# Filler products into an accumulators' bank and further into the program, and bulk loads entered by the modelled length of the DMA queue

## The chip, the cores and the metric

One core of a Trainium2 chip. The time is device microseconds of one execution of the whole program, median over several executions. The core's engines are TensorE (PE; its weight loads are listed as PEld), VectorE (DVE), ScalarE (ACT), GpSimd (POOL) and SyncE (SP, which here issues every DMA). Each engine runs its own list of instructions in order, and waits on semaphores where it needs another's result.

## The reference

Three stages over 4 batches of 768 tokens, 384 channels:

```python
# 1. linear attention with decay, 8 heads of 48: state (48 x 48) per head
cur = einsum('bhd,bhe->bhde', u[None] * kt, vt)
y[:, :, t] = einsum('bhd,bhde->bhe', rt, state + cur)
state = w[None, :, :, None] * state + einsum('bhd,bhe->bhde', kt, vt)
...
# 2. gated block, mixing over tokens
h = gelu(x @ w_in);  u, v = h[..., :512], h[..., 512:]
v_n = (v - mean) / sqrt(var + 1e-06) * g_ln
v_s = einsum('ts,bsd->btd', w_sg, v_n) + b_sg[None, :, None]
x = x + (u * v_s) @ w_out
...
# 3. causal convolution of 5 taps as a gate
gate = sigmoid(conv5(x));  out = (gate * (x @ w_val)) @ w_out
```

Weights of the second and third stage come as 64-bit floating point words and are turned into a sum of two narrower parts on the chip; every product with them is three matmuls (high by high, high by low, low by high).

## The kernel before

**Attention** goes by chunks of 128 tokens, 24 of them (6 a batch). Chunk i has, on PE: T (`att_T`, L551: transposes of r and of the scaled k, `ks`), S (`S_products`, L575: scores), KV (`KV_products`, L608), dT (L643), the product with the state (L651) and Y (L666: scores by v). DVE turns the transposed r and, for chunk 0, k into `rT` and `kT` (L559; later `kT` is ACT's, L557) and masks the scores (`sc`, L583). POOL makes `ks` (L497) and the diagonal term (`dv`, L526, L527, L535). ACT copies Y to `yT` (L683); SP writes it to a DRAM tile `xd` (L687, L688) and reads it back turned as `xf` (L693), from which ACT and DVE make the two parts of x (`R`, L721 and L725).

**The gated block** of a batch goes by V (6 row blocks, L824 to L826, `pm<-win,R` with 512 columns), U (`pm<-R,win`), SG (`pm<-wsg,vh`), O1 (`pm<-R,wout`), VAL (`pm<-R,w_val`) and O2 (`pm<-w_out,R`). Below, V(4) is V of row block 4 of batch 0, and so on.

**Weights.** `prepare` loads a block of 64-bit words (`Rst`, L351) and turns it: ACT reads the words first (`warm<-Rst`, L339, into a scratch in PSUM, `pw`), DVE does L340 to L342, then the two parts are written (L365, L373). `w_sg` is loaded as `st` (L393); ACT sums its squares (L397), `ssb` is the sum's copy (L409), and a small PE product with ones (`scale_w_sg`, L418) gives the scale by which `w_sg` is cast (`psg`, L447, L455) and transposed by DMA (L450). `load_conv` (L266) loads the convolution's taps as words, `cwd`, in three DMAs of 5 KB; ACT's first step on them is `cwt<-cwd` (L339).

**The order** of every engine's list is made when the program is built, by a planner with a clock of its own in modelled ns. PE takes the next ready task of two streams (attention and block); every other piece of work is a step of a *chain*, with the engines that may do it, a cost, a priority and what it needs. `next_step` picks the step that can start first, then by priority, `advance` writes it into its engine's list. `"Q"` is SP's list; `self.dma` is the time at which the modelled DMA queue runs empty. Where no PE task is ready, `go` moves the clock to the next event and writes filler products (bf16 ones by ones, 128 columns, result never read) for a share of the gap. Filler products keep PE from standing still, and nothing else. The tile that they write is `warm`: before, the columns from `TH` = 384 on of the bank `pw`, the same bank whose first 384 columns are the words' scratch. PSUM has 8 banks here: `pw`, four `pa` for attention, three `pm` for the block's accumulators.

Of the kernel before, what the change touches and what calls it, by code (L numbers as in the profile page):

```python
# [6 lines left out]
F32 = mybir.dt.float32  # L7
# [10 lines left out]
P = 128  # L18
# [8 lines left out]
TH = 384  # L27
# [4 lines left out]
class Kern:  # L32
# [28 lines left out]
    def mark(self, key, t=None):  # L61
        self.end[key] = self.pe_end + LAT if t is None else t

    def give(self, tok, n=1, t=None):
        self.tok[tok] += [self.pe_end + LAT if t is None else t] * n

    def chain(self, key, *steps, after=(), prio=1):

        self.left[key] = self.left.get(key, 0) + 1
        self.n_chain += 1  # L70
        self.chains.append([self.pe_end + LAT, prio, self.n_chain, key, list(steps), list(after)])

# [18 lines left out]
    def next_step(self):  # L91
        best = None
        for c in self.chains:
            engs, ns, f, *res = c[4][0]
            t = self.when(res[0] if res else (), c[5], c[0])
            if t is None:
                continue
            for e in engs:
                cost = step_ns(e, ns)
                s = max(t, self.free[e])  # L100
                if holds(e, engs, ns):
                    s = max(s, self.port)
                if e == "A" and isinstance(ns, tuple) and ns[0] != self.table:
                    s, cost = s + HOLD[ns[0]], cost + TURN
                k = (s, c[1], s + cost, c[2])
                if best is None or k < best[0]:
                    best = (k, c, e, cost)
        return best

    def advance(self, t):  # L110

        while True:
# [10 lines left out]
            if holds(e, engs, ns):  # L123
                self.port = s + cost
            c[0] = s + cost + LAT
            if e == "Q":
# [20 lines left out]
    def go(self, streams, choose):  # L147

        live = [[] for _ in streams]
        self.done = [0.0] * len(streams)  # L150
        while True:
            for n, (gens, window) in enumerate(streams):
                while len(live[n]) < window and gens:
                    g = gens.pop(0)
                    live[n].append([g, next(g)])
            if not any(live):
                return
            times = [[self.when(t[1][2], t[1][1], self.now) for t in ts] for ts in live]
            ready = [next((i for i, t in enumerate(ts) if t is not None and t <= self.now), None) for ts in times]
            n = choose(ready)  # L160
            if n is None:
                best = self.next_step()
                soon = [t for ts in times for t in ts if t is not None]
                if best is not None:
                    soon.append(max(best[0][0], self.now))
                assert soon, ("stuck", [t[1] for ts in live for t in ts], [(c[3], c[5], c[4][0][3:]) for c in self.chains])
                t = min(soon)
                for _ in range(int((t - self.now) * (FILL0 if self.now < 14000 else FILL) / (112 if self.now < 4000 else 56)) if self.now < FILL_END else 0):

                    nc = self.nc  # L170
                    nc.tensor.matmul(self.pw[:, TH:], self.onesb, self.onesb, start=True, stop=True)
                self.now = self.pe_end = t
                self.advance(self.now)
                continue
            i = ready[n]
            g, (ns, after, taken) = live[n][i]
            self.take(taken)
            self.pe_end = self.now + ns
            req = next(g, None)
            if req is None:  # L180
                live[n].pop(i)
            else:
                live[n][i][1] = req
            self.done[n] += ns
            self.now = self.pe_end
            self.advance(self.now)
# [26 lines left out]
    def consts(self):  # L213
        nc = self.nc
        self.ident = self.const([P, P], F32, "ident")
        make_identity(nc, self.ident)
        self.mask = self.const([P, P], BF16, "mask")
        nc.gpsimd.memset(self.mask, 1.0)
        nc.gpsimd.affine_select(
            out=self.mask, in_=self.mask, pattern=[[1, P]], base=-1, channel_multiplier=-1,  # L220
            compare_op=ALU.is_ge, fill=0.0,
        )
        self.exps = self.const([P, 1], F32, "exps")
        self.onesb = self.const([P, P], BF16, "onesb")
        nc.vector.memset(self.onesb, 1.0)

        nc.scalar.copy(self.exps, self.onesb[:, 0:1])
        nc.vector.memset(self.exps, -0.5)
        self.rp = [self.const([P, H, 64], F32, f"rp{i}") for i in range(NL)]
        self.kp = [self.const([P, H, D], F32, f"kp{i}") for i in range(NL)]  # L230
        self.ks = [self.const([P, H, 64], F32, f"ks{i}") for i in range(2)]
        for t in self.rp + self.ks:
            nc.vector.memset(t[:, :, D:], 0.0)
        self.junk = self.const([P, H, D], BF16, "junk")
        self.dvp = [self.const([P, H, 64], F32, f"dv{i}") for i in range(2)]
        for t in self.dvp:
            nc.gpsimd.memset(t[:, :, D:], 0.0)
        self.T = [self.const([HR, NP, HR], F32, f"T{i}") for i in range(2)]
        for t in self.T:
            nc.gpsimd.memset(t, 0.0)  # L240
        if WARM:

            self.pw = self.pa.tile([P, 512], F32, tag='pw', name='warm', bufs=1)
            for _ in range(WARM):
                nc.tensor.matmul(self.pw[:, TH:], self.onesb, self.onesb, start=True, stop=True)

    def load_w(self):
        nc = self.nc
# [864 lines left out]
    def run(self):  # L1113
        nc = self.nc
# [16 lines left out]
        for i in range(B * NCH):  # L1131
            self.att_new(i)
        self.chain("small", ("Q", (2, 1300), lambda e: self.load_small()), prio=2, after=[("ld", AFTER_SM)])
        self.chain("conv", ("Q", (12, 1100), lambda e: self.load_conv()), prio=2, after=[("ld", AFTER_CW), "small"])
        self.prepare_sg(PR_SG)
        for i in range(NCH):
            self.parts_sg(i, PR_PS)
# [25 lines left out]
def step_ns(e, n):  # L1163

    if isinstance(n, float):
        return n
    if e == "Q":
        return 1175.0 if n[0] == "T" else 475.0 * n[0]
    if isinstance(n, dict):
        return n[e]  # L1170
    if isinstance(n, tuple):
        return n[1]
    return {"V": 69 + 1.042 * n, "A": 93 + 0.833 * n, "P": 165 + 2.06 * n}[e]
# [14 lines left out]
AFTER_SG, AFTER_SM, AFTER_CW = 6, 6, 9  # L1188
WA, WM = 3, 4
NW = 3  # L1190
NR, NS, NA, NX, NY, NL, NV, NPA = 12, 10, 3, 3, 2, 3, 2, 4
WARM = 1
LAT = 130.0
A_FIRST, M_FIRST, RATE = 29000.0, 15000.0, 0.43
TOKENS = {"R": NR, "W": NW, "S": NS, "A": NA, "xf": NX, "yT": NY, "sc": 2, "pw": 1, "pa": NPA, "pm": 7 - NPA}
# [4 lines left out]
HOLD_G, HOLD_S, TURN = 200.0, 0.0, 1280.0  # L1200
HOLD = {"gelu": HOLD_G, "sigmoid": HOLD_S}
FILL, FILL0 = 0.4, 0.8
FILL_END = 9000.0
TAIL = [(1, 0, 0), (1, 0, 1), (1, 0, 2), (0, 1, 0), (0, 1, 1), (0, 1, 2), (2, 0, 0), (2, 0, 1), (1, 1, 0), (1, 1, 1), (1, 1, 2), (2, 0, 2), (2, 1, 0), (2, 1, 1), (2, 1, 2)]
W_LEAST, W_MOST = 0.75, 1.0
N_OK = HR * NP
# [42 lines left out]
```

## Time and profile before

| | |
|---|---|
| three executions | 470.57 us median (470.04 to 470.74) |
| profiled execution | 471.12 us, its span 469.4 us, mean granted clock 0.981 |
| PE | 445.6 us busy, 95% of the span, 3365 matmuls |
| DVE | 348.6 us, 74% |
| ACT | 204.7 us, 44% |
| POOL | 200.2 us, 43% |
| DMA | 41.35 MB |

The span runs from the first to the last instruction; the profiled execution's own time is 1.7 us longer. The granted clock is the share of TensorE's full clock (2.4 GHz) that the chip grants it; 0.50 is the lower of its two levels, 1.2 GHz. A busy share over the whole span is an average over a start in which PE is short of work and a long rest in which it is not.

### The profile page before, as it was taken

How to read it: one execution, taken by the hardware profiler on the slowest of the kernel's cores; microseconds unless marked ns; L12 is line 12 of the kernel's file. 1: busy time of each engine (PE TensorE's matmuls, PEld its weight loads, DVE VectorE, ACT ScalarE, POOL GpSimd, SP SyncE). 2: the span in 40 equal slices, each digit the busy share in tenths (PEclk: the TensorE clock that was granted, in tenths of full speed). 3: DMA queues.
4: the chain of work that ended last, by engine and by line, in shares of the span. 5: the costliest groups of instructions: out<-in, count | busy, mean ns of one | idle time of the engine just before them, and what ended most of it. 6: DMA issues, size and time to landing. Idle time of an engine off the chain costs nothing.

```text
span 469.4 us, 8848 instructions
## 1 busy us (share of the span) xinstructions
PE 445.6 (95%) x3365; PEld 378.6 (81%) x3365; DVE 348.6 (74%) x687; ACT 204.7 (44%) x441; POOL 200.2 (43%) x236
## 2 busy tenths in 40 slices
PE   6988987999998999999999998999999999999996
PEld 6776876968876999887877997987777989777895
DVE  7598958899998685677687766765488684559982
ACT  3547498725452465443143434741123374203142
POOL 4778375635469016664753364644011121300000
PEclk9799898999999899999999999999999999999999
DMA  7999975886243325332223333300000301000002
GB/s 149 234 228 229 268 214 112 172 201 168 53 85 67 103 52 135 85 73 49 52 50 86 103 68 92 94 1 0 3 1 19 116 0 52 0 2 0 1 34 73
DMA packets 116272, 41.35 MB, mean 88 GB/s; under 512 B 89344, under 2 KB 114048, under 8 KB 116224
## 3 DMA queue, kind: packets, MB, share of 16 engines
q1 hardware_dynamic: 116224, 40.73, 35.9%
q8 instruction: 28, 0.46, 0.4%
q14 instruction: 20, 0.16, 0.1%
HBM read 28.92 MB, written 9.44 MB: 82 GB/s over the span
## 4 chain that ended last, share of the span: by engine, by line
PE 72%; DVE 12%; DMA 4%; POOL 3%; ACT 3%; issue 3%; SPq 1%; DVEq 0%; POOLq 0%; ACTq 0%
PE pm L824 20%; PE pm L825 19%; PE pm L826 19%; PE pa L575 4%; PE pa L666 3%; PE pa L551 3%; PE pa L651 2%; DVE R L725 2%; DVE sc L583 1%; DVE warm L945 1%; DMA cwd<-in_moe_conv_w_dram 1%; DMA Rst<-in_moe_w_in_dram 1%; PE pa L608 1%; DVE S L340 1%; DVE S L341 1%
## 5 line engine op out<-in xcount | busy, mean ns | idle before, releaser
L824 PE MATMUL pm<-wsg,vh 128*128 128x384 f16 x192 | 62.8, 327 | 0.5 <-DVE S L911 0.5
L826 PE MATMUL pm<-wsg,vh 128*128 128x384 f16 x192 | 62.6, 326 | 0.0
L825 PE MATMUL pm<-wsg,vh 128*128 128x384 f16 x192 | 62.6, 326 | 0.0
L945 DVE SCALAR_TENSOR_TENSOR warm<-xf,cw,warm 128x384 f32<-128x384 f32 x72 | 44.6, 619 | 7.2 <-ACT warm L943 5.9
L623 ACT ACTIVATE T<-T,W 112x112 f32<-112x112 f32 x80 | 27.0, 383 | 32.2 <-DVE T L617 32.0
L497 POOL TENSOR_TENSOR ks<-kp,tabS 128x384 f32<-128x384 f32 x24 | 24.5, 1020 | 37.2 <-PE pa L608 31.7
L911 DVE SCALAR_TENSOR_TENSOR S<-pm,gs,b_bc 128x384 f32<-128x384 f32 x32 | 19.7, 616 | 22.9 <-PE pm L826 22.7
L825 PE MATMUL pm<-R,wout 128*128 128x384 f32 x96 | 32.9, 343 | 1.5 <-DVE R L889 1.4
L824 PE MATMUL pm<-R,win 128*128 128x384 f32 x96 | 34.4, 358 | 0.0
L824 PE MATMUL pm<-R,wout 128*128 128x384 f32 x96 | 34.2, 357 | 0.0
L850 POOL TENSOR_TENSOR rs<-rs,exps 128x1 f32<-128x1 f32 x24 | 13.3, 556 | 48.6 <-DVE rs L847 48.5
L881 ACT ACTIVATE S<-pm 128x384 f32<-128x384 f32 x32 | 15.7, 490 | 41.9 <-PE pm L826 37.4
L826 PE MATMUL pm<-R,wout 128*128 128x384 f32 x96 | 32.5, 339 | 0.0
L575 PE MATMUL pa<-rT,kT 48*128 48x128 f32 x384 | 29.0, 291 | 3.6 <-ACT kT L557 1.7
L826 PE MATMUL pm<-R,win 128*128 128x384 f32 x96 | 32.3, 336 | 0.0
L825 PE MATMUL pm<-R,win 128*128 128x384 f32 x96 | 32.3, 336 | 0.0
L889 POOL TENSOR_TENSOR R<-xf,R 128x384 fp32r<-128x384 f32 x10 | 10.1, 1013 | 50.6 <-ACT R L1177 30.1
L863 DVE BATCH_NORM_STATS2 bst<-A 128x6 f32<-128x512 f32 x24 | 16.6, 692 | 18.9 <-ACT A L862 18.7
L824 PE MATMUL pm<-win,R 128*128 128x512 f32 x72 | 30.3, 421 | 0.0
L824 PEld LDWEIGHTS <-vh 128*128 128x128 f16 x192 | 18.7, 98 | 13.5 <-issue 2.7
L575 PEld LDWEIGHTS pa<-rT,kT 48*128 48x128 f32 x384 | 24.4, 193 | 6.5 <-ACT kT L557 3.0
L826 PEld LDWEIGHTS <-vh 128*128 128x128 f16 x192 | 18.8, 98 | 12.7 <-DVE vh L868 0.4
(181 smaller groups left out, 1272.1 us busy)
## 6 DMA issues: line engine op xcount, KB each, us to landing
rp<-in_r_dram SPq DMA_DIRECT2D x24, 192.0 KB, 3.4
kp<-in_k_dram SPq DMA_DIRECT2D x24, 192.0 KB, 3.9
v<-in_v_dram SPq DMA_DIRECT2D x24, 192.0 KB, 3.0
xd<-yT SPq DMA_DIRECT2D x48, 96.0 KB, 2.2
xf<-xd SPq DMA_DIRECT2D x24, 192.0 KB, 2.5
out_dram<-S SPq DMA_DIRECT2D x24, 192.0 KB, 1.9
Rst<-in_moe_w_in_dram SPq DMA_DIRECT2D x8, 384.0 KB, 5.3
Rst<-in_moe_w_out_dram SPq DMA_DIRECT2D x7, 384.0 KB, 5.1
```

The source lines that it names most:

```text
L497: e.tensor_mul(t[:, :, 0:D], kp, self.tabS)
L551: nc.tensor.transpose(pt[:HR, p * P:(p + 1) * P], sv[:, p * P:p * P + HR], self.ident)
L575: nc.tensor.matmul(ps[:, p * P:(p + 1) * P], kT[r0:r0 + D, p, :], rT[r0:r0 + D, p, :], start=True, stop=True)
L623: return lambda e: e.activation(tnew[:, p, :], tnew[:, p, :], AF.Copy, scale=self.W[:, p:p + 1])
L666: nc.tensor.matmul(py[r0:r0 + w, p * P:(p + 1) * P], vt[:, (2 * p + j) * D:(2 * p + j) * D + w], sc[j][:, p, :], start=not own and not c a ...
L824: nc.tensor.matmul(ps, lh, rh, start=m == 0, stop=False)
L825: nc.tensor.matmul(ps, lh, rl, start=False, stop=False)
L826: nc.tensor.matmul(ps, ll, rh, start=False, stop=m == total - 1)
L863: ("V", 602.0, lambda e: e.bn_stats(st, ge)),
L881: self.chain(("u", b, half, f), ("A", ("gelu", 371.0), lambda e: e.activation(t, pu[:, :TH], AF.Gelu_apprx_tanh), [], ["pm"]))
L911: ("V", 529.0, lambda e: e.scalar_tensor_tensor(t, pg[:, :TH], self.gs[:, d:d + 1], self.b_bc[:, ts], ALU.mult, ALU.add), [], ["pm"]),
L945: eng.scalar_tensor_tensor(t, row[:, j:j + TH], self.cw[:, e, j:j + 1], t, ALU.mult, ALU.add)
```

## The change

Four edits. Filler products write a tile of the `pm` pool (`pf`) that is taken at the start and never read, instead of columns of `pw`. They go on to a modelled time of 30,000 ns (before: 9,000), at the share `FILL` = 0.4 of a gap past 14,000. A step of SP's list with a priority above 0 (weights, chunks from the seventh on, small tables, outputs) starts in the plan no earlier than 2,500 ns before the modelled queue runs empty. And the taps' load costs 5 units in the plan instead of 12.

```diff
                 if holds(e, engs, ns):
                     s = max(s, self.port)
+                if e == "Q" and c[1] > 0:
+                    s = max(s, self.dma - AHEAD)
...
-                    nc.tensor.matmul(self.pw[:, TH:], self.onesb, self.onesb, start=True, stop=True)
+                    nc.tensor.matmul(self.pf[:, 0:P], self.onesb, self.onesb, start=True, stop=True)
...
-            self.pw = self.pa.tile([P, 512], F32, tag='pw', name='warm', bufs=1)
+            self.pw = self.pa.tile([P, 512], F32, tag='pw', name='words', bufs=1)
+            self.pf = self.pm.tile([P, 512], F32, tag="pm", name="warm")
             for _ in range(WARM):
-                nc.tensor.matmul(self.pw[:, TH:], self.onesb, self.onesb, start=True, stop=True)
+                nc.tensor.matmul(self.pf[:, 0:P], self.onesb, self.onesb, start=True, stop=True)
...
-        self.chain("conv", ("Q", (12, 1100), lambda e: self.load_conv()), prio=2, after=[("ld", AFTER_CW), "small"])
+        self.chain("conv", ("Q", (5, 1100), lambda e: self.load_conv()), prio=2, after=[("ld", AFTER_CW), "small"])
...
+AHEAD = 2500.0
...
-FILL_END = 9000.0
+FILL_END = 30000.0
```

Because the planner's clock decides every list, the lists differ from there on. PE has 64 more rows (32 filler products with their weight loads). From the second batch on PE's lists agree again but for numbers of buffers.

PE's list at the start. Before, the transposes of `tabK` are followed at once by the scores of chunk 0 (`rT`, `kT`), KV, T and dT, and Y (`sc`, `v`):

```order
L326 MATMUL pa_291<-ident,tabK 128x112 x4
L575 MATMUL pa_304<-rT_288,kT_298 128x128
L575 MATMUL pa_305<-rT_288,kT_298 128x128
...
L608 MATMUL pa_320<-v_143,ks_123 48x48 x8
L551 MATMUL pa_332<-ident,rp_118 112x128 x4
L643 MATMUL pa_341<-ident,dv_131 112x128 x4
L666 MATMUL pa_341<-sc_329,v_143 48x128
```

PE's list at the same place with the change (lines are 3 further down; `warm` is now the `pm` tile):

```order
L329 MATMUL pa_289<-ident,tabK 128x112 x4
L173 LDWEIGHTS onesb
L173 MATMUL warm<-onesb 128x128
...
L578 MATMUL pa_314<-rT_286,kT_301 128x128
L578 MATMUL pa_315<-rT_286,kT_301 128x128
...
L611 MATMUL pa_332<-v_144,ks_123 48x48 x8
L554 MATMUL pa_344<-ident,rp_118 112x128 x4
L646 MATMUL pa_353<-ident,dv_131 112x128 x4
L173 LDWEIGHTS onesb
L173 MATMUL warm<-onesb 128x128
L669 MATMUL pa_353<-sc_341,v_144 48x128
```

Fourteen filler products stand between the transposes of `tabK` and the scores of chunk 0, and one ahead of Y; 16 more follow up to the dT of chunk 2, and one stands ahead of all these.

PE's list around the small product for the scale of `w_sg` (`ssb`), before: behind the transposes of chunk 7 and dT of chunk 6, ahead of the nine products of V(4) (`R_851` to `R_853`):

```order
L551 MATMUL pa_1031<-ident,ks_124 112x128 x4
L643 MATMUL pa_1038<-ident,dv_131 112x128 x4
L418 LDWEIGHTS onesb
L418 MATMUL pm_1063<-ssb,onesb 128x12
L824 MATMUL pm_1077<-win_96,R_851 128x512
L825 MATMUL pm_1077<-win_97,R_851 128x512
...
L666 MATMUL pa_1038<-sc_898,v_773 48x128
```

The same place with the change:

```order
L554 MATMUL pa_1074<-ident,ks_124 112x128 x4
L646 MATMUL pa_1083<-ident,dv_131 112x128 x4
L827 MATMUL pm_1089<-win_96,R_898 128x512
...
L829 MATMUL pm_1089<-win_96,R_900 128x512
L421 LDWEIGHTS onesb
L421 MATMUL pm_1121<-ssb,onesb 128x12
L669 MATMUL pa_1083<-sc_935,v_816 48x128
```

The product that waits for `ssb` has gone behind the nine of V(4).

SP's list around the taps (`cwd`), before: they stand ahead of the write of chunk 5's rows (`xd_63<-yT_1050`):

```order
L351 DMA Rst_891<-in_moe_w_out_dram 128x768
L393 DMA st_185<-in_moe_w_sg_dram 128x768 x3
L266 DMA cwd<-in_moe_conv_w_dram 128x5x2 x3
L693 DMA xf_778<-xd_62 128x3x128
L351 DMA Rst_1002<-in_moe_w_out_dram 128x768
L483 DMA rp_118<-in_r_dram 128x8x48
L483 DMA kp_121<-in_k_dram 128x8x48
L687 DMA xd_63<-yT_1050 48x4x128
L688 DMA xd_63<-yT_1050 48x4x128
L693 DMA xf_778<-xd_63 128x3x128
```

The same place with the change (`yT_1038` is chunk 5's):

```order
L396 DMA st_186<-in_moe_w_sg_dram 128x768
L486 DMA v_1001<-in_v_dram 128x8x48
L354 DMA Rst_1016<-in_moe_w_out_dram 128x768
L354 DMA Rst_1027<-in_moe_w_out_dram 128x768
L690 DMA xd_63<-yT_1038 48x4x128
L691 DMA xd_63<-yT_1038 48x4x128
L269 DMA cwd<-in_moe_conv_w_dram 128x5x2 x3
L486 DMA rp_118<-in_r_dram 128x8x48
L486 DMA kp_121<-in_k_dram 128x8x48
L696 DMA xf_827<-xd_63 128x3x128
```

The taps now stand behind the two writes of chunk 5, which wait for its `yT`. Earlier on the same list, the loads of r and k of chunk 3 have gone ahead of two of the three `w_in` blocks that stood in a row before them.

## Rows read from the trace of the kernel before

**Rows 1.** Busy us by stretch: PE, PEld, DVE, ACT, POOL, then clock, DMA share, GB/s.

```profile
12.00:18.00 6.00, 6.00 (x56) 5.00 (x52) 2.66 (x5) 2.16 (x7) 5.85 (x7) 0.50 1.00 261
20.00:57.00 37.00, 31.40 (x338) 26.65 (x339) 34.58 (x70) 19.48 (x50) 24.41 (x26) 0.95 0.99 236
69.00:81.00 12.00, 7.97 (x71) 6.36 (x71) 9.69 (x29) 10.04 (x28) 6.55 (x9) 0.86 0.54 121
81.00:155.00 74.00, 70.65 (x586) 57.17 (x586) 67.52 (x112) 36.45 (x77) 45.05 (x45) 1.00 0.55 121
155.00:160.00 5.00, 5.00 (x22) 5.00 (x21) 2.70 (x6) 1.52 (x4) 0.00 (x0) 0.67 0.47 146
```

**Rows 2.** PE's timeline, 10 to 27 us: start, us, instruction, idle before it.

```profile
10.95 0.22 PE L171 MATMUL warm<-onesb 128*128 128x128 bf16 x1 [2.09 <-ACT warm L339]
...
11.48 2.04 PE L575 MATMUL pa<-rT,kT 48*128 48x128 f32 x16
...
16.15 1.95 PE L666 MATMUL pa<-sc,v 128*48 128x128 f32 x16
18.03 0.80 PE L551 MATMUL pa<-ident,ks 128*112 128x128 f32 x4
...
20.01 1.43 PE L575 MATMUL pa<-rT,kT 48*128 48x128 f32 x16
21.37 0.65 PE L551 MATMUL pa<-ident,ks 128*112 128x128 f32 x4
22.75 1.16 PE L575 MATMUL pa<-rT,kT 48*128 48x128 f32 x16 [0.73 <-ACT kT L557]
...
25.79 1.08 PE L666 MATMUL pa<-sc,v 128*48 128x128 f32 x16
```

**Rows 3.** DVE's timeline, 10 to 14 us.

```profile
10.31 0.36 DVE L340 TENSOR_SCALAR S<-Rst 128x384 int32<-128x384 int32 x1 [0.54 <-DMA Rst<-in_moe_w_in_dram]
10.58 0.68 DVE L559 TENSOR_TENSOR kT<-pa,tabK 112x512 f32<-112x512 f32 x1
...
13.55 1.29 DVE L583 TENSOR_TENSOR sc<-pa,mask 128x512 f32<-128x512 f32 x2 [0.86 <-PE pa L575]
```

**Rows 4.** ACT's and POOL's timelines, 11 to 23 us.

```profile
11.59 0.48 ACT L328 COPY tabS<-pa 128x384 f32<-128x384 f32 x1 [0.69 <-PE pa L326]
...
22.11 0.59 ACT L557 COPY kT<-pa 112x512 f32<-112x512 f32 x1 [0.96 <-PE pa L551]
...
12.15 1.00 POOL L497 TENSOR_TENSOR ks<-kp,tabS 128x384 f32<-128x384 f32 x1 [1.91 <-ACT tabS L328]
...
15.82 1.00 POOL L497 TENSOR_TENSOR ks<-kp,tabS 128x384 f32<-128x384 f32 x1
...
21.32 1.00 POOL L497 TENSOR_TENSOR ks<-kp,tabS 128x384 f32<-128x384 f32 x1 [1.59 <-PE pa L575]
```

**Rows 5.** SP's timeline, the three `w_in` blocks, and the writes of one chunk's rows.

```profile
11.89 3.04 SPq L351 DMA_DIRECT2D Rst<-in_moe_w_in_dram  x3
...
71.10 0.33 SPq L687 DMA_DIRECT2D xd<-yT  x1
71.48 0.44 SPq L688 DMA_DIRECT2D xd<-yT  x1
```

**Rows 6.** PE's timeline, 60 to 72 us.

```profile
60.16 0.40 PE L824 MATMUL pm<-win,R 128*128 128x512 f32 x1
...
62.23 0.34 PE L824 MATMUL pm<-R,win 128*128 128x384 f32 x1
...
71.83 0.17 PE L418 MATMUL pm<-ssb,onesb 128*128 128x12 bf16 x1 [2.90 <-ACT ssb L409]
```

**Rows 7.** The tile of the taps: who touches it, when, and its DMAs' landing.

```profile
L266 SPq DMA_DIRECT2D cwd<-in_moe_conv_w_dram x3: 864/1133/1348, 58.8 to 61.4; - x3
...
L339 ACT ACTIVATE cwt<-cwd x1: 208/208/208, 72.1 to 72.1; 128x15 f32<-128x15 f32 x1
...
DMA to landing us min/median/max: 4.4/5.4/6.6
```

## The prediction

> **What bounds the kernel now.** I read the busy times by stretch first [rows 1]. From 81 us on PE is the bound: 70.65 of the 74 us to 155 are busy, at full clock but for 155 to 160. An order that leaves PE's work alone can win there only what PE waits, 3.35 us, and what the clock of 0.67 costs, 0.33 of 5 us or 1.65. Before 81 us it is otherwise. From 12 to 18 us PE counts as busy throughout, but at a clock of 0.50, so three of the six microseconds are lost. From 20 to 57 us DVE is busy 34.58 of 37 us and PE 31.40: there DVE sets the pace, and work that starts earlier stays earlier by as much. From 69 to 81 us PE is busy 7.97 of 12 us at a clock of 0.86: 4.03 us idle and 0.14 of 12, 1.7 us, of slow clock.
>
> Then the timelines, for what ends those waits. PE stands 2.09 us in front of a filler product, which waits for ACT's first read of weight words into the same bank [rows 2]; the scores behind it take 2.04 us where the same sixteen take 1.16 at full clock. In the later stretch the longest wait is 2.90 us for `ssb` [rows 6], and the slow clock follows it.
>
> **The change part by part.**
>
> *The bank.* With its own bank no filler product waits for ACT. That does not bring chunk 0's scores forward much: they need `kT`, which stands on DVE behind a step that waits for the first weight block's DMA, and ends at 10.58 + 0.68 = 11.26 us [rows 3] in either kernel. What moves is `tabS`: PE's transposes of `tabK` no longer stand behind the wait, so ACT's copy, which waited 0.69 us for them [rows 4], follows its word read, and POOL's first `ks`, at 12.15 us, starts 0.7 us earlier.
>
> *Fourteen filler products ahead of the scores, and the clock.* They fill the time until 11.26. I take it that the clock then stays at full through 12 to 18 us. The path, from the rows: scores 11.3 to 12.4 (1.16); masks 1.29, with DVE's own steps in between to 14.0 [rows 3]; Y 1.08 to 15.1 [rows 2]. Before, Y ran from 16.15 to 18.1, and the transposes of chunk 1's `ks` at 18.03. Now these hit another floor: POOL is busy 5.85 of the 6 us [rows 1], and its `ks` of chunk 1 ends at 16.82 [rows 4], less the 0.7, at 16.1. Transposes 0.65 to 16.8, ACT's `kT` 0.59 to 17.4, and chunk 1's scores start at about 17.5 instead of 20.01: **2.5 us earlier**. Bounds: nothing, if the clock falls all the same; 3.1 us, if POOL were no floor (3.0 from the clock of 0.50 and 0.1 of start). I take 2.5, since POOL's floor is read off its own rows.
>
> *32 more filler products.* The one ahead and the fourteen lie in waits. Seventeen more stand among real work until the dT of chunk 2. At full clock one costs at most what a real product of as many columns does per pass, a sixteenth of 1.16 us, 0.07; all of them 1.2 us, nothing if they fall in waits. PE has 5.6 us of idle time in 20 to 57 (37 less 31.40), so I take 0.3.
>
> *Loads by the modelled queue.* Three `w_in` blocks took SP 3.04 us to issue [rows 5]; two now stand behind chunk 3's r and k. In the old order POOL waited 1.59 us before `ks` of chunk 3, at 21.32 [rows 4]; that wait would have eaten 2.5 us of progress by PE, and with the loads about 2 us earlier (two thirds of 3.04) it does not. I give it no gain of its own: 0, bounds 0 and 1.6. The blocks that move back are those that no product asks for yet; DVE's steps on them come later by one or two chunks in its list too. From 20 to 57 us nothing in DVE's list shrinks, so the 2.5 us are carried, neither more nor less.
>
> *The product that waits for `ssb`.* It goes behind the nine products of V(4). Nine of that kind take 2.07 us at full clock (60.16 to 62.23, rows 6). About as many ACT instructions stand ahead of `ssb` as before, so it is as late as before within PE's work, and of the 2.90 us 0.8 stay. With so short a wait I expect no slow clock behind it: 2.1 + 1.7, **3.8 us won**. Bounds: 0 and 4.6 (2.90 + 1.7).
>
> *The taps.* This is the part that costs. In the old order the third of their DMAs starts at 61.4 us and lands 4.4 to 6.6 later, at 68 at the latest; ACT asks at 72.1 [rows 7]: 4 us of cover. Now they start behind the writes of chunk 5's rows. From the end of `yT`: 0.8 us for the two writes (71.10 to 71.92, rows 5), 2.6 to the third's start (58.8 to 61.4), 5.4 to its landing [rows 7]: 8.8 us. In ACT's list 18 instructions lie between `yT` and the step that reads the taps (three casts of x, four squares of two instructions, two copies of U, `ssb`, two of V, `kT`, one of words); at ACT's mean in 69 to 81 us, 10.04 us by 28 or 0.36 [rows 1], that is 6.5. ACT then stands **2.3 us**, and behind it wait a normalisation, the first cast of `w_sg` and chunk 6's `yT`, whose bank PE needs for its next transposes. Bounds: 1.3 and 3.5 by the landings, 0 if ACT is late anyway, 5.2 if the clock falls behind the wait (1.7 more). I take 2.3.
>
> The Trainium skill (DMA: Bandwidth & Descriptors, Latency and other measured facts) says that the access to HBM is the main part of a DMA's fixed cost and shrinks under lighter load. By that the taps, which now go out when most of the bulk has landed, would come well under 5.4 us, ACT would not stand at all, and the sum below would end at 464.6. No row of before has the taps under light load, so I stay with 5.4.
>
> *81 us and later.* The lists differ up to the second batch, with the same work. I leave the 5 us lost there as they are.
>
> **Sum.** Against the profiled execution, 471.12: less 2.5, plus 0.3, less 3.8, plus 2.3, is 3.7 less, 467.4. The three runs' median is 0.55 below the profiled one; the prediction for a median is 470.57 less 3.7, **466.9**.
>
> **The rivals.**
>
> *A: the start is won and lost again at the taps.* If ACT's stand is followed by a slow clock, it costs 2.3 + 1.7 = 4.0, and eats what `ssb` gives; if the chunks' `ks` then also wait as at 21.32, only 0.9 of the 2.5 stay: 470.57 + 0.2 - 0.9 + 0.3, **470.2**, no change that shows. For it: POOL and DVE are both near full in the stretches between. Against: the loads for `ks` go out earlier.
>
> *B: the filler products don't hold the clock.* The old list's fall came after 2.09 us without a product [rows 2], and the new one has gaps as well, POOL's floor from 15.1 to 16.1 for one. Then 2.5 becomes about 0.7, from POOL alone: **468.7**. The Trainium skill (TensorE: Matmul & The Clock Gate, Part 1) says that the chip's look at PE's activity runs free of the kernel, so that one kernel may change level at different places in different runs. By that B would hold in some executions and not in others, with 1.8 us between them; the three runs of before, 0.15% apart, show no such spread.
>
> *C: slower.* In the stretch to 160 us the new order puts SG's second to fourth columns and two thirds of O1(0,0) and O1(0,1) in one piece with no attention between, and later lets O2 and O1 alternate. The parts of the gated values and of x that they read are made one behind the other on DVE and POOL. DVE is busy 67.52 of 74 us there [rows 1]. The old order pays 5 us for such waits and the slow clock that follows. One more of that kind costs about as much; the point from which it decides is 4.6 us (the 3.7 won and 0.9, 0.2%) beyond the old loss. Six microseconds more, the old loss a second time and a little, gives **473**.
>
> *D: more is won.* The waits of 81 to 160 us vanish, since attention runs ahead of the block: 466.9 less 5 is **462**. Nothing in the profile speaks for it but that they were made by one order.
>
> **How the numbers follow.** This kernel's runs tell apart about 0.2%, 0.9 us. Forecast, 462.9 to 469.8: 0.52. A: 0.13. B: 0.08. C: 0.18. D: 0.09. Faster takes the forecast, D and B (which ends 1.9 under the median) with 0.01 off for what of them falls short: 0.68; same is A less what of it strays: 0.12; slower is C and those strays: 0.20. The range reaches down over half of D's distance, to 463.0, and up over A to 471.8, where C begins; what is outside, most of C and half of D, is some 0.2. The forecast's own range comes from the bounds: 470.57 less (3.1 + 4.6), 462.9, to 470.57 less 2.5 less 3.8 plus 5.2 plus 0.3, 469.8.
>
> **What would show it.** Right: in the profile after, the clock is 1.00 in 12 to 18 us, no PE wait names ACT's `words`, the second group of scores starts near 17.5 us, the wait for `ssb` is under 1 us, and ACT stands 1 to 4 us before `cwt<-cwd`. Wrong: a clock of 0.50 somewhere in 10 to 20 us; a wait for `ks` or for a chunk's r and k of over 1 us in 15 to 57; no wait at the taps; or, if C holds, waits of PE in 81 to 200 us of over 8 us together with a clock below 1.00.

## The result, and the profile after

The changed kernel took 464.66 us (median of four, 463.91 to 467.04), the kernel before 470.31 beside it: ratio 0.9889, 95% interval 0.9849 to 0.9929. That is 5.7 us faster; 3.7 were predicted, and 464.66 lies in the range. A median is taken over all runs, while a ratio leaves out the runs more than 1.5% above the fastest of their kernel, so the two need not agree to the last digit. The profiled execution took 465.4 us, its span 463.7 (before 469.4). The total came near by luck: three errors cancelled in part, as the same views show. Line numbers are one to five higher in the kernels below than in the rows of before.

Busy time by stretch of the changed kernel, columns as in [rows 1]:

```profile
12.00:18.00 6.00, 4.72 (x73) 3.62 (x69) 2.48 (x6) 3.92 (x10) 5.38 (x6) 1.00 1.03 219
20.00:57.00 37.00, 29.79 (x314) 24.36 (x316) 31.16 (x63) 20.49 (x51) 25.14 (x28) 0.95 0.91 220
69.00:81.00 12.00, 8.91 (x85) 7.00 (x83) 10.85 (x31) 10.54 (x27) 9.26 (x11) 1.00 0.74 142
81.00:155.00 74.00, 72.76 (x586) 61.02 (x585) 66.21 (x119) 37.61 (x80) 42.22 (x42) 1.00 0.59 126
155.00:160.00 5.00, 5.00 (x49) 4.45 (x48) 3.52 (x7) 2.10 (x4) 3.04 (x3) 1.00 0.20 42
```

The clock is 1.00 in 12 to 18 us, as forecast. 69 to 81 us has lost its slow clock in this execution, 81 to 155 us stands 1.24 us idle instead of 3.35, and 155 to 160 us runs at full clock. In 20 to 57 us the clock is 0.95 as before.

PE's timeline of the changed kernel, beside [rows 2] and [rows 6]:

```profile
18.02 1.16 PE L578 MATMUL pa<-rT,kT 48*128 48x128 f32 x16
...
20.48 1.16 PE L578 MATMUL pa<-rT,kT 48*128 48x128 f32 x16 [0.51 <-ACT kT L560]
...
28.21 0.65 PE L554 MATMUL pa<-ident,rp 128*112 128x128 f32 x4 [2.56 <-ACT yT L686]
...
30.49 1.91 PE L654 MATMUL pa<-rT,T 112*112 112x128 f32 x8
...
36.78 0.47 PE L827 MATMUL pm<-win,R 128*128 128x512 f32 x1
...
57.81 0.44 PE L827 MATMUL pm<-R,win 128*128 128x384 f32 x1
...
72.47 0.18 PE L421 MATMUL pm<-ssb,onesb 128*128 128x12 bf16 x1
...
76.14 0.65 PE L554 MATMUL pa<-ident,rp 128*112 128x128 f32 x4 [1.03 <-ACT yT L686]
78.05 0.62 PE L554 MATMUL pa<-ident,ks 128*112 128x128 f32 x4 [1.26 <-POOL nm L854]
...
78.86 0.47 PE L827 MATMUL pm<-win,R 128*128 128x512 f32 x1
```

Chunk 1's scores start at 18.02 (before 20.01), chunk 2's at 20.48 (before 22.75): 2.0 and 2.3 us earlier. Then PE stands 2.56 us for `yT`, and the product with the state takes 1.91 us, at half clock. U(0,0), the first `pm<-R,win`, starts at 57.81; in the trace of before at 57.01. Nothing of the start's gain is left there. The product for `ssb` waits for nothing. V(5) starts at 78.86 (before 80.86).

The gain was gone before the clock fell. In before, chunk 3's transposes came at 27.66, 0.55 us earlier than the 28.21 above:

```profile
27.66 0.65 PE L551 MATMUL pa<-ident,rp 128*112 128x128 f32 x4 [0.79 <-DVE sc L583]
```

DVE's timeline shows where it went. The changed kernel, then before:

```profile
20.41 0.95 DVE L343 TENSOR_SCALAR S<-Rst 128x384 int32<-128x384 int32 x1
...
23.72 1.08 DVE L343 TENSOR_SCALAR S<-Rst 128x384 int32<-128x384 int32 x1
24.72 1.35 DVE L376 TENSOR_TENSOR win<-S,win 128x384 fp32r<-128x384 f32 x1
```

```profile
22.50 0.35 DVE L340 TENSOR_SCALAR S<-Rst 128x384 int32<-128x384 int32 x1
...
24.87 0.35 DVE L340 TENSOR_SCALAR S<-Rst 128x384 int32<-128x384 int32 x1
25.13 0.55 DVE L373 TENSOR_TENSOR win<-S,win 128x384 fp32r<-128x384 f32 x1
```

DVE comes to the first of these steps on `w_in` 2.09 us earlier than before, but the three take 3.38 us instead of 1.25, and one sum for chunk 3's diagonal term (L518, 0.54 us) stands among them as well. In the changed trace a step of POOL's is running when each of the three begins (from 20.12, 23.57 and 24.54 on, 1.0 to 1.1 us each); in before POOL is idle when the first two begin, and beside the third it begins a step of its own that takes 1.44 us. That a step of one engine holds up the other's is a reading of these times, not tested by a run.

The tile of the taps, changed kernel, beside [rows 7]:

```profile
L269 SPq DMA_DIRECT2D cwd<-in_moe_conv_w_dram x3: 439/524/612, 69.0 to 70.2; - x3
L342 ACT ACTIVATE cwt<-cwd x1: 207/207/207, 73.2 to 73.2; 128x15 f32<-128x15 f32 x1
...
DMA to landing us min/median/max: 2.2/2.3/2.5
```

The taps landed by 72.7, and ACT, at 73.2, did not stand for them.

Two events cut the execution into three parts: U(0,0)'s first product and V(5)'s. In us:

| part | before | changed | difference | predicted |
|---|---|---|---|---|
| to U(0,0) | 57.01 | 57.81 | +0.8 | -2.2 (2.5 less 0.3) |
| U(0,0) to V(5) | 23.85 | 21.05 | -2.8 | -1.5 (3.8 less 2.3) |
| V(5) to the end of the span | 388.54 | 384.84 | -3.7 | 0 |

### The profile page after: what moved, and what is told of

The parts are those of the page before. It is cut to its first block, busy times and chain, and to the rows that moved or that the text cites. A ratio compares the mean times of both kernels' runs of the same rounds, so it can differ in the third digit from the quotient of the medians.

```text
span 463.7 us, 8893 instructions
## 1 busy us (share of the span) xinstructions
PE 442.0 (95%) x3397; PEld 375.1 (81%) x3397; DVE 343.4 (74%) x686; ACT 202.3 (44%) x439; POOL 203.2 (44%) x237
## 4 chain that ended last, share of the span: by engine, by line
PE 74%; DVE 11%; ACT 3%; POOL 3%; issue 2%; DMA 1%; DVEq 0%; SPq 0%; POOLq 0%; ACTq 0%
PE pm L827 20%; PE pm L829 20%; PE pm L828 20%; PE pa L669 4%; PE pa L578 3%; PE pa L554 3%; PE pa L654 3%; DVE sc L586 1%; DVE words L948 1%; ACT junk L400 1%; DVE R L728 1%; PE pa L611 1%; DVE psg L458 1%; DVE S L344 1%; DMA v<-in_v_dram 1%
## 5 line engine op out<-in xcount | busy, mean ns | idle before, releaser
L948 DVE SCALAR_TENSOR_TENSOR words<-xf,cw,words 128x384 f32<-128x384 f32 x72 | 44.6, 619 | 7.2 <-ACT words L946 6.0
L827 PE MATMUL pm<-R,wout 128*128 128x384 f32 x96 | 33.6, 350 | 0.3 <-DVE S L914 0.3
L853 POOL TENSOR_TENSOR rs<-rs,exps 128x1 f32<-128x1 f32 x24 | 13.9, 581 | 45.4 <-DVE rs L850 43.1
L828 PE MATMUL pm<-R,wout 128*128 128x384 f32 x96 | 32.5, 339 | 0.4 <-POOL R L892 0.4
L829 PE MATMUL pm<-R,wout 128*128 128x384 f32 x96 | 32.3, 337 | 0.0
L827 PE MATMUL pm<-win,R 128*128 128x512 f32 x72 | 29.9, 416 | 0.5 <-ACT S L884 0.5
L829 PEld LDWEIGHTS <-vh 128*128 128x128 f16 x192 | 18.8, 98 | 12.7 <-DVE vh L871 0.4
L829 PE MATMUL pm<-win,R 128*128 128x512 f32 x72 | 28.5, 395 | 0.3 <-DVE R L728 0.3
L578 PE MATMUL pa<-rT,kT 48*128 48x128 f32 x384 | 27.9, 285 | 0.9 <-ACT kT L560 0.5
L828 PE MATMUL pm<-win,R 128*128 128x512 f32 x72 | 28.5, 395 | 0.0
```

The costliest lines, as they stand in the source:

```text
L578: nc.tensor.matmul(ps[:, p * P:(p + 1) * P], kT[r0:r0 + D, p, :], rT[r0:r0 + D, p, :], start=True, stop=True)
L827: nc.tensor.matmul(ps, lh, rh, start=m == 0, stop=False)
L828: nc.tensor.matmul(ps, lh, rl, start=False, stop=False)
L829: nc.tensor.matmul(ps, ll, rh, start=False, stop=m == total - 1)
L948: eng.scalar_tensor_tensor(t, row[:, j:j + TH], self.cw[:, e, j:j + 1], t, ALU.mult, ALU.add)
```

## The experiments

Theory 1, formed from this table: the gain is the order of the lists, and the start's gain is lost on the way to U(0,0). Theory 2 is the prediction's: the start's gain is carried. Twelve kernels ran, four to a chip, each group beside its own runs of the kernel before; medians are compared through the ratio to those. The last columns are each profile's: the three parts, and PE's idle time in 81 to 160 us (79 less its busy time there).

| kernel | median us | ratio (interval) | U(0,0) | to V(5) | to end | idle |
|---|---|---|---|---|---|---|
| before | | | 57.01 | 23.85 | 388.54 | 3.35 |
| changed | 464.66 | 0.9889 (0.9849 to 0.9929) | 57.81 | 21.05 | 384.84 | 1.24 |
| e1 start alone | 469.87 | 0.9962 (0.9926 to 0.9998) | 56.43 | 23.77 | 385.80 | 2.70 |
| e2 order alone | 465.20 | 0.9899 (0.9870 to 0.9927) | 57.74 | 21.04 | 384.82 | 1.28 |
| e3 short fill | 467.13 | 0.9910 (0.9876 to 0.9944) | 59.71 | 21.80 | 384.49 | 1.03 |
| e4 taps 12 | 467.39 | 0.9928 (0.9903 to 0.9953) | 58.09 | 21.83 | 384.28 | 0.00 |
| e5 gap filled | 464.77 | 0.9893 (0.9852 to 0.9934) | 56.63 | 21.15 | 385.22 | 0.97 |
| e6 load at taps | 466.10 | 0.9935 (0.9893 to 0.9978) | 56.60 | 21.04 | 384.46 | 1.00 |
| e7 ssb late | 473.90 | 1.0102 (1.0068 to 1.0135) | 55.17 | 21.01 | 394.62 | 8.30 |
| e8 AHEAD 4000 | 471.90 | 1.0039 (1.0006 to 1.0073) | 58.20 | 17.08 | 393.82 | 8.16 |
| e9 AHEAD 2000 | 474.59 | 1.0068 (1.0035 to 1.0100) | 59.88 | 19.00 | 395.52 | 8.29 |
| e10 AHEAD 3000 | 467.17 | 0.9941 (0.9916 to 0.9967) | 58.63 | 19.04 | 387.43 | 2.54 |
| e11 waits filled | 468.75 | 0.9977 (0.9950 to 1.0005) | 59.61 | 26.46 | 383.83 | 2.17 |
| e12 changed again | 466.34 | 0.9895 (0.9859 to 0.9930) | 58.29 | 21.80 | 384.51 | 0.33 |

**e1, the start alone.** Each engine's real work stands in the order of before; only the fillers are new.

```diff
-                    nc.tensor.matmul(self.pw[:, TH:], self.onesb, self.onesb, start=True, stop=True)
+                    nc.tensor.matmul(self.pf[:, 0:P], self.onesb, self.onesb, start=True, stop=True)
...
-FILL_END = 9000.0
+FILL_END = 30000.0
```

> The kernel before with the filler products in their own bank and running to 30,000 modelled ns, and nothing else: every engine's real work stands in the same order as before. Theory 1 (the order of the lists brings the gain; what is won at the start is lost again before 57 us, where DVE paces): 469.8 to 471, U(0,0)'s first product within 0.6 us of 57.0, the ssb wait and the slow clock at 155 to 160 us still there. Theory 2 (the start as the prediction had it, 2.5 less 0.3, is carried to the end): 468.1, U(0,0) at 54.8. In both the clock is 1.00 in 12 to 18 us.

U(0,0) started 0.6 us earlier, the median lies in theory 1's range, and the wait for `ssb` is there (2.92 us); but the clock in 155 to 160 us was 1.00, so that slow stretch does not belong to the old order as such. The ratio makes the start worth 1.8 us of 470, with 0.1 and 3.5 as ends, so theory 2's 2.2 is not ruled out by the time. In this profile the clock fell to 0.50 in 24 to 26 us, so a part of the start's gain may have gone there. By itself e1 doesn't decide, but it is a third of what the whole change gave.

**e2, the order alone.**

```diff
+                if e == "Q" and c[1] > 0:
+                    s = max(s, self.dma - AHEAD)
...
-        self.chain("conv", ("Q", (12, 1100), lambda e: self.load_conv()), prio=2, after=[("ld", AFTER_CW), "small"])
+        self.chain("conv", ("Q", (5, 1100), lambda e: self.load_conv()), prio=2, after=[("ld", AFTER_CW), "small"])
```

> The loads by the modelled queue and the taps' 5 units alone, with the old fillers in the words' bank up to 9,000 modelled ns: real work in the order of the changed kernel. Theory 1: 464 to 466, as the changed kernel. Theory 2: 466.9 to 468, since it lacks the 2.2 of the start. If the bank matters only with the new order, it lies between.

This ratio is the changed kernel's. One window of e2, then two rows of its PE timeline:

```profile
12.00:18.00 6.00, 6.00 (x55) 4.97 (x54) 2.52 (x5) 2.09 (x6) 6.00 (x7) 0.50 0.97 214
```

```profile
29.43 0.65 PE L553 MATMUL pa<-ident,rp 128*112 128x128 f32 x4 [2.70 <-DVE sc L585]
...
36.71 0.48 PE L826 MATMUL pm<-win,R 128*128 128x512 f32 x1
```

Without the new fillers the clock is 0.50 in 12 to 18 us, and chunk 1's scores come at 19.90; but V(0) starts at 36.71, in the changed kernel at 36.78. From there the two traces agree within 0.1 us down to O2 of the first batch (141.57 and 141.62). So the order alone is enough, and in it the start adds nothing that these runs show. DVE's steps point to the order as well: the two steps shown above at 23.72 and 24.72 us take 1.14 and 1.35 us in e2, 1.09 and 1.35 in e6, but 0.57 and 0.55 in e1, which has the old order.

**e3, the bank without the longer fill**, `FILL_END = 9000.0` in the changed kernel.

> The changed kernel with the fillers ending at 9,000 modelled ns as before, in their new bank: 62 filler products fewer. Theory 1: within 0.9 us of the changed kernel's 464.7. Theory 2: about 466.5, since without the fillers ahead of the first scores the clock falls in 12 to 18 us and 1.8 of 2.5 go.

The clock was 0.51 in 12 to 18 us: the bank alone doesn't hold it there. The median is nearer to theory 2's 466.5, and U(0,0) came 1.9 us later than in the changed kernel's profile; but the ratio overlaps e2's, which lacks both the bank and the fill. Undecided.

**e4, the taps at 12 units**, `(5, 1100)` back to `(12, 1100)` in the changed kernel.

> The changed kernel with the taps' load at 12 units again: the lists are the same up to the step behind the taps (they stand behind the same two writes), and differ from there to 160 us, where the next read of the turned rows comes ahead of the loads of r and k. If the 3.7 us won in 81 to 160 us belong to the new order as such: 464 to 466. If they hang on this one sequence: 467 to 471, with PE waits of more than 3 us in 81 to 160 us. No stand of ACT ahead of the taps in either case, as none is in the changed kernel.

Inconclusive as a time: 467.39 is in the second range, without the waits that should go with it. PE is never idle in 81 to 160 us:

```profile
81.00:160.00 79.00, 79.00 (x635) 66.77 (x634) 70.07 (x127) 38.82 (x81) 44.93 (x45) 0.98 0.55 120
```

So another sequence than the changed kernel's covers that stretch as well (at a clock of 0.98, 1.6 us of 79). e4 lacks the taps' units and is still 0.7% faster than before, clear of the interval, so the pacing of the loads brings most of the gain; whether the units bring the rest is open. Why the median lies 1.3 us above the profiled run (466.06) was not found.

**e5, the wait at 28 us filled.** The changed kernel with

```diff
-(FILL0 if self.now < 14000 else FILL)
+(FILL0 if self.now < 14000 else 5.5 * FILL if 23900 < self.now < 25200 else FILL)
```

> The changed kernel with 38 more filler products behind Y of chunk 2, where PE stands 2.56 us for ACT's yT; real work in the same order. If the slow clock behind that wait is what eats the 1.9 us won at the second scores: clock 1.00 in 28 to 33 us, chunk 3's scores at 32.0 to 32.7 (33.52 in the changed kernel), U(0,0)'s first product at 56.6 to 57.0 (57.81), the time 0.8 to 1.2 us under the changed kernel's. If DVE and ACT set the pace there whatever PE's clock: scores at 33.2 or later, U(0,0) at 57.5 to 57.8, no change in the time.

```profile
25.52 2.52 PE L173 MATMUL warm<-onesb 128*128 128x128 bf16 x42
28.50 0.65 PE L554 MATMUL pa<-ident,rp 128*112 128x128 f32 x4 [0.46 <-ACT yT L686]
...
30.36 1.04 PE L654 MATMUL pa<-rT,T 112*112 112x128 f32 x8
```

In the trace it went as the first theory said: the state's product takes 1.04 instead of 1.91, the scores come at 32.34, U(0,0) at 56.63. The time did not follow: the clock fell at another place instead, in 69 to 81 us:

```profile
69.00:81.00 12.00, 9.62 (x78) 7.70 (x79) 10.82 (x30) 10.58 (x25) 9.57 (x11) 0.86 0.83 145
```

And e6, whose PE list is the changed kernel's, has the wait too (2.57 us), but no slow clock at 28 us, and reaches U(0,0) at 56.60 without these fillers. So the fall in the first profile belongs to that execution, not to the wait alone.

**e6, the queue loaded ahead of the taps.** In `load_conv` of the changed kernel:

```diff
+            for k in range(2):
+                nc.sync.dma_start(self.bulk[k], self.w_sg[k * P:(k + 1) * P, :])
```

> The changed kernel with two more DMAs of 393 KB each (rows of w_sg, copied to a DRAM tile that nothing reads) just ahead of the taps on SP; all other lists the same. If the taps landed in 2.2 to 2.5 us because the queue was nearly empty: landing 4 to 6 us now, ACT stands 1.5 to 3 us ahead of its first step on the taps, V(5)'s first product moves from 78.9 to 80 to 81.5, the time 1 to 2.5 us longer. If a 5 KB DMA of small pieces lands in 2.5 us whatever else is under way: no stand of ACT, no change in the time. The loads behind it on SP (r and k of chunk 9) come later by the same in either case, with one more chunk of cover.

Tile of the taps, then PE's timeline:

```profile
L271 SPq DMA_DIRECT2D cwd<-in_moe_conv_w_dram x3: 524/582/758, 69.4 to 70.6; - x3
...
  DMA cwd<-in_moe_conv_w_dram: 1.5, 1
...
DMA to landing us min/median/max: 3.0/3.4/3.9
```

```profile
75.89 0.65 PE L556 MATMUL pa<-ident,rp 128*112 128x128 f32 x4 [1.99 <-ACT yT L688]
76.83 0.62 PE L556 MATMUL pa<-ident,ks 128*112 128x128 f32 x4 [0.29 <-POOL nm L856]
...
77.64 0.48 PE L829 MATMUL pm<-win,R 128*128 128x512 f32 x1
```

The landing depends on the load, and ACT stood 1.5 us, against the second theory. But V(5) did not move as the first one had it: the wait for `yT` grew from 1.03 to 1.99, and the one for `nm` behind it shrank from 1.26 to 0.29. From U(0,0) to V(5) it is 21.04 us, as in the changed kernel: the stand cost PE nothing. The ratios of e5 and e6 overlap, so their times decide nothing here.

**e7, the product for the scale held back.** The kernel before with

```diff
-        yield 30, ["ssb", "small"], ["pm"]
+        yield 30, ["ssb", "small", "V4"], ["pm"]
...
             self.three(pv, (x[0][:, cs], x[1][:, cs], wh[:, c, FF:], wl[:, c, FF:]), (c, NC))
+        if (b, i) == (0, 4):
+            self.mark("V4")
```

> The kernel before, with the small product for the scale of w_sg held back until V(4) is done, and nothing else by hand (the planner's order of DVE's, ACT's and POOL's steps differs a little from there on). The prediction's step: of 5.7 us lost in 69 to 81 us 3.8 come back, V(5)'s first product at about 77.1 instead of 80.86, the time about 467. Rival: ACT, busy 10 of 12 us there, is late with the next thing too, so that V(5) starts at 79.5 or later and the time is 469.5 to 470.5.

From U(0,0) to V(5) it took 21.01 us, as if e7 had won the changed kernel's 2.8. It did not win them in the same way. e7's V(4):

```profile
69.47 0.50 PE L824 MATMUL pm<-win,R 128*128 128x512 f32 x1 [2.38 <-ACT R L721]
```

With the product for `ssb` out of the way V(4) still stands 2.38 us, now for `R`, its own operand from ACT, and the slow clock follows as before (0.86 in 69 to 81 us). Up to V(4) only 0.5 us are won, 14.30 against 14.84. ACT's timelines show why. Before, then changed:

```profile
70.51 0.57 ACT L683 COPY yT<-pa 112x512 f32<-112x512 f32 x1
70.97 0.70 ACT L721 CAST R<-xf 128x128 fp32r<-128x128 f32 x3
71.58 0.20 ACT L409 CAST ssb<-ss 128x12 bf16<-128x12 f32 x1
```

```profile
66.87 0.57 ACT L686 COPY yT<-pa 112x512 f32<-112x512 f32 x1
67.34 0.70 ACT L724 CAST R<-xf 128x128 fp32r<-128x128 f32 x3
...
71.01 0.20 ACT L412 CAST ssb<-ss 128x12 bf16<-128x12 f32 x1
```

Before, and in e7, `yT` and `R` stand in ACT's list behind all the squares of `w_sg` and end just ahead of `ssb`; in the changed kernel they stand ahead of the last four squares. The other 2.3 us that e7 has at V(5) are a matter of order: V(5) goes ahead of the transposes of `ks` and dT, which in before stand ahead of it (dT with a wait of 0.77) and in e7 follow from 84.58 us on. So e7 does not show the prediction's step; the rival, ACT late with the next thing as well, held at V(4). (V(5) came at 76.18, earlier than either expectation, but U(0,0) was 1.8 us early here.)

And e7 is the slower kernel: 6 us more from V(5) on. The planner answered the one held-back task with other lists on every engine from there on, in which PE stands 8.30 us in 81 to 160 us. Its longest waits there:

```profile
PE pa L551 <- DVE sc L588: 2.1, 2, 1.7
PE pm L824 <- DVE S L977: 1.0, 1, 1.0
PE pa L643 <- DVE sc L583: 0.9, 1, 0.9
```

**e8, AHEAD 4000**, one constant of the changed kernel.

> The changed kernel with bulk loads entering 4,000 modelled ns ahead of the queue's end instead of 2,500; another order of all lists up to 160 us. If pacing the loads brings the gain as such: 464 to 466. If the gain belongs to the sequence that 2,500 happens to give: 467 to 471, with PE waits of over 4 us in 57 to 160 us.

Slower too: pacing the loads as such isn't the gain. Its PE waits in 81 to 160 us are of the same kind as e7's:

```profile
PE pm L827 <- DVE S L978: 2.0, 1, 2.0
PE pa L646 <- DVE sc L586: 1.5, 1, 1.5
PE pa L554 <- ACT yT L686: 1.3, 1, 1.3
```

In both, PE has attention in long pieces there with no product of the block between: by the traces, waits included, the two longest take 13.8 and 12.7 us in e7 and 17.6 and 7.8 in e8, in the changed kernel 5.7 and 4.7. (The expectation of e9 timed the same pieces from the lists and made them shorter, in the same order.) PE then waits for masks and `yT` of the same few chunks, and later the block waits for DVE's `S` with no attention left beside it. That reading was tested on two kernels chosen by their lists.

**e9 and e10, AHEAD 2000 and 3000.**

> The changed kernel with bulk loads entering 2,000 modelled ns ahead of the queue's end. Read from PE's list alone, and timed by the rows of the changed kernel (products of a shape by their spacing), attention stands between the product for the scale of w_sg and the second batch in pieces of up to 8.6 and 7.1 us with no product of the block between; in the changed kernel the longest are 3.6 and 3.6, in the kernel before 3.6 and 3.1, in e7 8.1 and 5.6, in e8 9.2 and 5.0. If long pieces of attention are what costs (PE then waits for the masks, kT and T of the same few chunks, and the block later has no attention beside it): 471 to 474, PE idle for over 6 us in 81 to 160 us. If it is the nearness of AHEAD to 2,500, or fewer loads at a time, that counts: 464 to 467.

> The changed kernel with 3,000 instead of 2,500: the longest pieces of attention by the same reading are 3.6 and 2.5 us. If long pieces of attention are what costs: 463.5 to 467.5, PE idle for under 3 us in 81 to 160 us. If only the sequence that 2,500 gives is good: 469 to 473.

Windows of e9, then of e10:

```profile
81.00:160.00 79.00, 70.71 (x589) 56.70 (x588) 67.27 (x131) 38.16 (x80) 46.71 (x45) 1.00 0.61 122
```

```profile
81.00:160.00 79.00, 76.46 (x628) 64.15 (x627) 68.37 (x123) 38.48 (x81) 43.46 (x42) 1.00 0.59 127
```

Both came out nearly as the list said: 8.29 and 2.54 us idle, 474.59 (0.6 above its range) and 467.17 us; the longest pieces in the traces are 13.9 us in e9 and 7.3 in e10. Part of e9's time is the clock, 0.79 in 20 to 57 us of its profile: its two runs at a mean clock of 0.996 and 0.999 took 469.6 and 469.5, still about 2.5 more than e10's at 0.999. The time is not smooth in the constant. No run changed the length of the pieces alone, so this is a reading that foretold two kernels, not a cause taken apart. e10 is 0.5% behind the changed kernel's ratio in the same group (e12), with intervals that overlap.

**e11, more waits filled.** As e5, with `2.5 * FILL` from 62,000 modelled ns on and `FILL_END = 84000.0`.

> The changed kernel with 38 more filler products behind Y of chunk 2 (as in e5) and 13, 2 and 19 more ahead of the waits near 76 and 78 us; real work in the same order. If the spread of the runs comes from a clock that falls behind PE's waits in some executions: clock 1.00 from 12 us on in the profile, runs closer together than the changed kernel's beside it (463.5 to 467), median 463.3 to 464.2. If the waits are no cause of the spread: median and spread as the changed kernel's.

The first theory was wrong: slower than e12, clear of the intervals, and not closer together (466.89 to 471.68, where e12 ran 463.82 to 466.90). Even its run at a mean clock of 0.999 took 466.89; e12 took 463.82 at 0.993. PE's timeline shows one way in which fillers cost:

```profile
72.06 0.44 PE L827 MATMUL pm<-R,win 128*128 128x384 f32 x1 [2.71 <-ACT S L884]
...
81.31 0.90 PE L173 MATMUL warm<-onesb 128*128 128x128 bf16 x13
```

The thirteen that were meant for the wait near 76 us ran at 81.31, behind a wait at another place, and cost 0.90. How much of the rest is theirs stays open: the clock fell in 20 to 26 us of this execution too, and the wait of 2.71 us, for ACT's `S`, has no match in the changed kernel.

**e12, the changed kernel again.**

> The changed kernel once more, beside the others on one chip: 463.9 to 467, and in its profile a slow clock in one stretch, none, or another one than at 28 to 33 us if the level that the chip grants behind a wait is not fixed by the kernel.

Faster by 1.05% (1.11% in the first result). Its windows show the clock falling in other stretches than in the first profile as well as in the same:

```profile
20.00:57.00 37.00, 29.76 (x316) 24.30 (x314) 31.61 (x64) 20.52 (x51) 25.12 (x27) 0.95 0.96 230
...
69.00:81.00 12.00, 9.20 (x84) 7.82 (x83) 10.83 (x31) 10.05 (x26) 8.33 (x11) 0.86 0.72 135
81.00:155.00 74.00, 73.67 (x582) 61.97 (x581) 64.98 (x118) 38.70 (x82) 43.07 (x42) 0.98 0.61 128
```

No kernel was faster than the changed one by more than the intervals.

## Why the prediction was right in its total and wrong in its terms

*The bank and the clock, 2.5 us.* Right as far as chunk 1's scores: 2.0 us earlier, 17.5 forecast and 18.02 measured, with POOL's `ks` as the floor (PE waited 1.28 us for it at 16.36). The clock was 1.00 in 12 to 18 us in all ten profiles with the longer fill, 0.50, 0.50, 0.51 and 0.72 in the four without. Rival B is not out for that: in e9 and e11, which have the fill, the clock fell right behind PE's wait for that `ks` (1.72 and 1.97 us), to 0.50 in 20 to 26 us, and chunk 1's scores, which took 2.08 us, started 0.8 and 1.0 us earlier than before, near the 0.7 that B gave. So B held in those two executions and not in the others. What failed in the changed kernel's profile is "the 2.5 us are carried". The prediction had DVE as the pace from 20 us on and its list as fixed; but three of DVE's steps grew by 2.1 us in all, so the lead was gone at chunk 3's transposes (28.21, before 27.66). Against e2, which has the same order without the fillers, the changed kernel is 1.9 us ahead at chunk 1's scores and 1.2 at chunk 3's transposes (28.21 and 29.43): on the way one of DVE's steps on `w_in` took 0.95 us (20.41 to 21.36), 0.35 in e2. The 1.2 go to the slow clock at 28 us; without it (e5, e6) 1.1 us reach U(0,0). The other 0.7 by which U(0,0) is late against before is the new order's: e2 starts it at 57.74 with the old start.

*32 fillers, 0.3.* Not seen separately: e5 has 38 more and the same time. With e11's 34 more at later places the kernel was slower; how much of that is theirs is open.

*Loads by the modelled queue, "no gain of its own: 0".* This step failed most. The new order of the loads, with the taps' units, changes every list, and e2, which has both without the fillers, has the whole gain.

*The product for `ssb`, 3.8 less, and the taps, 2.3 more.* Together 1.5 less; 2.8 less was measured from U(0,0) to V(5): 2.4 up to V(4) (12.47 against 14.84), 0.4 behind it. The wait (2.90 to 0.51) came out as forecast, but the step that was to bring it did not: the prediction put the whole 2.90 down to `ssb` and did not ask what else V(4) needed from ACT. It needed `R`, which ended 0.1 us before `ssb`; moving the product alone is worth 0.5 us (e7). What took the wait away is that ACT's new list makes `yT` and `R` ahead of the last squares. That the term fits in size is luck. The slow clock did not come behind V(4), but the waits for `yT` and `nm` (1.03 and 1.26) came up further on, and in e12, e3, e4 and e5, with the same order so far, the clock fell there instead; in e12 the stretch took 21.80 us, 2.05 less than before. The taps' term was 0. The landing was sized from a loaded queue, 5.4 us, and was 2.3. The Trainium skill (DMA: Bandwidth & Descriptors, Latency and other measured facts) says that the fixed cost shrinks under lighter load; the trace agrees, with 2.2 to 2.5 us at 17 to 94 GB/s (68 to 72 us) against 4.4 to 6.6 at 260 to 353 (58 to 64 us, before), and 3.0 to 3.9 in e6. Whether the memory or the earlier transfers of the queue hold them back, these runs do not separate. The sum that the prediction gave for that rule, 464.6, met the measured 464.66 by luck, as its other terms were off. And the landing was only half of it: where ACT did stand, 1.5 us in e6, PE's next wait hid it. The prediction priced a stand of ACT as a delay of PE without asking what PE would have waited for anyway.

*81 us and later, "I leave the 5 us lost there as they are".* Wrong by 3.7 us between these two profiles, of which 1.65 are the slow clock that before had in 155 to 160 us. Rival D was right there; it was given 0.09 since nothing in the profile spoke for it. The runs did: the seven other profiles that keep the changed kernel's order up to V(5) need 383.8 to 385.2 us from there on (e4 with another sequence), the two of the old order 388.5 (before) and 385.8 (e1, at a clock of 1.00 in 155 to 160). The old order's loss there varies from run to run, so by these profiles 0.6 to 4.7 us are the new order's. Rival C had the mechanism, block and attention each in one piece, but for other orders than this one: e7, e8 and e9 are 5 to 7 us worse in that part than before (in e7 some of it is the work that V(5) overtook).

*About 0.2% can be told apart.* Too fine. In the three groups the kernel before ran from 467.54 to 473.51 (25 runs), 464.23 to 472.66 (23) and 466.51 to 473.26 (29); the three runs on which the figure rested were too few.

Two of the signs of being wrong that the prediction named came up: no wait at the taps, and a wait for `ks` of over 1 us (1.28, the floor that its own sum had).

## What to carry to other kernels

Where a planner's clock writes the lists, a changed constant is a new draw of every list behind it: read the new list for long pieces of one stream before costing the edit's own steps, since here 500 modelled ns down cost 8 us and up 2, the 2 not clear of the intervals (by the ratios of e9, e10 and e12). A wait put down to one tile may hide another that ends just before it: look in the releasing engine's list for what else the waiting engine needs from it. A gain at the start counts only as far as the next place where another engine's list sets the date, so compare the two kernels there, at a product that both have. A stand of one engine is priced by what the next one would have waited for anyway.

## What the runs showed of the hardware

The clock falls at different places in executions of one PE list: in the changed kernel's first profile at 28 to 33 us alone, in e12 there and behind 76 us, in e6 nowhere up to 160 us. At 28 us a PE wait of 2.56 us was followed by the slow clock, one of 2.57 us in e6 was not. The Trainium skill (TensorE: Matmul & The Clock Gate, Part 1) says that the chip's look at PE's activity runs free of the kernel; these rows agree. Across the 23 to 29 runs of the kernel before in each group the time falls with the mean clock (correlations -0.72 to -0.78), so a part of their spread of 6 to 8.4 us goes with it.
